# V cast into DRAM and loaded by SyncE; batch 1's global rows gathered one by one

## The chip, the cores and the metric

One core of a Trainium2 chip runs the whole kernel in one launch. The metric is the device time of that launch in microseconds. The kernel before took 402.18 us (median of three runs, 399.71 to 402.31).

## The reference

Sparse attention, followed by a two-layer feed-forward block with a "snake" activation:

```
scores = (q @ k^T) / sqrt(64)                    # q, k, v: 8 batches, 8 heads, 576 rows, 64 columns
mask   = |i - j| <= 32, or i is global, or j is global      # 8 global rows, given by global_idx
attn   = softmax(where(mask, scores, -1e9));  x = attn @ v  # x: 4608 tokens of 8 * 64 = 512
h      = x @ w_in                                # 512 -> 2048
g      = h + sin(alpha * h)**2 / (alpha + 1e-9)
out    = g @ w_out                               # 2048 -> 512, float32
```

## The kernel before

**Per batch.** `attention(b)` goes over four pairs of heads (`hp`; a pair is head hp and head 4 + hp, on the two halves of the partitions). For a pair it makes band scores in two halves (`scores`, L785, into the bank `ring`), an exponential on ScalarE (L794), a mask on VectorE (L795), the products of the weights with V (`products`, L823, key 0) and with ones (key 1, the row sums), and divides by way of a logarithm: ScalarE writes `L` (L849), SyncE stores a row of it to `LC` (L851), ScalarE makes the inverse (L858) and VectorE multiplies into `xT` (L861). `L` has two buffers. The products of a pair are two steps behind its scores. `gemm1(b)` multiplies `xT` with `w_in` in 16 groups of 128 columns (L1014), with sine (L1044), square (L1047 or L1049) and the sum into `H2` (L1050). `gemm2(b)` is a generator of single matmuls with `w_out` (L1062); `fill(n)` takes n of them wherever TensorE would otherwise have a gap: `START`, `FIRST` and `SECOND` say how many at the start of an attention and after the first and second half of a pair, `PER_GROUP` and its like how many in a group of `gemm1`. After 16 of them ScalarE copies a block to `osb` (L1068, three buffers) and SyncE stores it (L1075).

**Order.** Each engine works through its instructions in the order of the program, and a wait holds up all that stands behind it on that engine. The order is written out by hand: attention 0, then for each batch b the first GEMM of b and the attention of b + 1, in which the second GEMM of b fills the gaps. `beside(at)` places other work after pair `at` of an attention. A DMA is issued by POOL (its own queue, q0, which can also cast), SyncE or ScalarE (hardware queues, q1 and q10).

**What is loaded.** Keys and queries of batch b are cast to bfloat16 in DRAM by POOL (`cast_qk`, L322, the tiles `kd` and `qd`, two buffers each) and turned by SyncE's transposing DMA (`turn_qk`, L331, into `kt` and `qt`); VectorE copies them into `KX` and `QX` (`place`, L341 and L348), for batches 1 and 2 in groups 10 to 13 of the first GEMM. Batch 0 is loaded as it is and turned by TensorE. V rows go straight into `VX` by POOL's casting DMA (`load_v`, L400), 32 transfers of 168 rows a batch; for batches 0 and 1 two of the pairs are staged in float32 by SyncE (`stage_v`, L389) and cast by POOL (L393). `VX` holds 48 V rows and 8 rows of the global keys in each group of partitions; `load_vg` (L405) fills in the latter.

**Global rows.** For batch 0 three indirect DMAs of POOL (L560) fetch 64 rows each of v, k and q. For all others SyncE fetches them by `gather` (L503): eight row indices are loaded into registers (L499), and 24 transfers with a register in the address bring the rows of all batches for k, q and v. POOL casts them (`cast_kq`, L715, and `cast_globals_v`, L711, into `VGb`), TensorE turns keys and queries (`turn_kq`, L727), and POOL copies each batch's columns into `KX` and `QX` (`place_globals`, L360 and L364). `gather(k)` and `gather(q)` stand in the set-up, ahead of batch 1's `turn_qk`; `gather(v)` behind it.

**POOL and SyncE around batch 1.** POOL: `w_in` in two halves with `cast_qk(1)` in between, `cast_kq`, a tiny copy into `seen` that waits for `kt`, V of pair 0, `w_out` in four transfers, then (in program order in group 10 of the first GEMM) `cast_globals_v`, `place_globals(1)`, V of pair 1 and the casts of the staged pairs 2 and 3, then `cast_qk(2)` and V of batch 2. SyncE: the gathers of k and q, `turn_qk(1)`, the gather of v, the staging of pairs 2 and 3, `load_vg(1)`, the logarithm stores, `turn_qk(2)`.

The last part checks bounds on the inputs of sine and logarithm and would call `general_path` where they don't hold.

Of the kernel before, what the change touches and what calls it, by code (L numbers as in the profile page):

```python
# [246 lines left out]
def kernel(  # L247
# [56 lines left out]
    VG0 = main.tile([NG * B, D], DT.bfloat16, name="VG0")  # L304
    seen = main.tile([1, 1], DT.bfloat16, name="seen")
    girow = main.tile([1, NG], DT.int64, name="girow")
    grow = main.tile([NG * B, 1], DT.int32, name="grow")
    grow2 = main.tile([P, 1], DT.int32, name="grow2")
# [8 lines left out]
    def cast_qk(b):  # L317

        cast[b] = []
        for src, name in ((k, "kd"), (q, "qd")):  # L320
            t = dramp.tile([P, H * S * D // P], DT.bfloat16, name=name)
            nc.gpsimd.dma_start(  # L322
                out=t[:], in_=src[b].rearrange("h s d -> (h s d)").rearrange("(p f) -> p f", p=P)
            )
            cast[b].insert(0, t)

    def turn_qk(b):

        turned[b] = [trp.tile([P, H * HALF], DT.bfloat16, name=name) for name in ("qt", "kt")]
        for i in (1, 0):  # L330
            nc.sync.dma_start_transpose(  # L331
                out=turned[b][i][:], in_=cast[b][i][:].rearrange("p (r c) -> (p r) c", c=P)
            )
        del cast[b]
# [49 lines left out]
    def stage_v(b, hp, st):  # L384


        for t in range(2):
            for r, src in v_rows(b, t * NHP + hp):
                nc.sync.dma_start(out=st[r : r + 24, :, t, :], in_=src)  # L389
# [5 lines left out]
    def load_v(b, hps=range(NHP)):  # L395
        for hp in hps:
            for t in range(2):
                h = t * NHP + hp
                for r, src in v_rows(b, h):
                    nc.gpsimd.dma_start(out=VX[b % 2][r : r + 24, :, h, :], in_=src)  # L400

    def load_vg(b):
        src = VGb[b::B] if b else VGd[:]
# [15 lines left out]
    def load_w_out():  # L419
        for g in range(4):  # L420
# [11 lines left out]
    GKQ = [H2[0 : NG * B, nt, S : S + H * D] for nt in (0, 12)]  # L432
# [106 lines left out]
    nc.vector.tensor_copy(out=grow[:], in_=rowf[0 : NG * B, 4:5])  # L539
    for e in range(2):  # L540
# [81 lines left out]
    def place_global_keys(t, copy):  # L622
        copy(
            out=KX[0][t * D : (t + 1) * D, :, :, KT:NK],
            in_=pg[1][:].rearrange("p (j t h) -> p t h j", t=2, h=NHP)[:, t][:, :, None, :].to_broadcast(
# [4 lines left out]
    def place_global_queries(t, copy):  # L630
        for y in range(2):
            copy(
                out=globals_of(0, slice(t * D, (t + 1) * D), y),
                in_=pg[0][:].rearrange("p (x y t h) -> p t y h x", t=2, h=NHP, y=2)[:, t, y][
# [15 lines left out]
    load_registers()  # L650
    gather(k, gk)
    gather(q, gq)
# [52 lines left out]
    stage1 = [  # L705
# [522 lines left out]
```

## Time and profile before

| | |
|---|---|
| Three runs | 402.31, 402.18, 399.71 us |
| Profiled execution | 398.96 us, span 397.2 us |
| Busy, share of the span | TensorE 85%, VectorE 69%, ScalarE 68%, POOL 47% |
| Mean granted TensorE clock | 0.959 |
| POOL's V transfers (L400) | 224 issues, 141.8 us busy |
| DMA queue q0 (POOL) | 58176 packets, 18.67 MB, 41.6% of 16 engines' span |
| DMA queue q1 (SyncE) | 47210 packets, 20.54 MB, 25.8% |

The span is from the first to the last instruction; the time has some 1.8 us around it. Busy time of TensorE is that of matmuls. A row of the list of waits gives who waited, for whom, then the microseconds in total, how often, and the longest. A row in order of time gives start and duration in microseconds, engine (SPq is SyncE's queue), line, operation, what is written and read, how many were merged, and in brackets the idle time before and what ended it. A row of a queue gives packets, megabytes and the time that the packets took as a share of 16 engines in the stretch.

### The profile page before, as it was taken

What the parts mean: (1) busy time and instruction counts of PE and PEld (TensorE: products, weight loads), DVE (VectorE), ACT (ScalarE), POOL (GpSimd) and SP (SyncE); (2) the same over time, 40 slices, a digit from 0 to 9 for tenths busy, and PEclk for the clock granted to TensorE, in tenths of its full rate; (3) what the DMA queues carried; (4) which work ended last, traced back from release to release, by engine and by line L of the source; (5) the groups of instructions that cost most, each with busy time, mean ns of one, the idle gap of its engine ahead of it and who ended that gap; (6) DMA issues with size and microseconds to landing.
All of it is one profiled execution on the core that took longest, in us unless ns stands there. A gap on an engine that the chain in (4) does not pass through costs nothing. (4 is left out here: it accounts for less than half of the span.)

```text
span 397.2 us, 11426 instructions
## 1 busy us (share of the span) xinstructions
PE 336.1 (85%) x4564; PEld 209.6 (53%) x4564; DVE 274.9 (69%) x521; ACT 269.7 (68%) x387; POOL 185.2 (47%) x300
## 2 busy tenths in 40 slices
PE   1576955299979999989999999899999998999990
PEld 1554633146645565556555755466556555665450
DVE  3554884247868788958897889588968785768520
ACT  1566893168777778768877797588787876777510
POOL 7880186657967958948749905980000000000001
PEclk9998995589999999999999999899999999999997
DMA  7999789899899898979966994596111011001221
GB/s 121 106 154 183 122 110 188 127 169 129 103 182 133 114 177 92 133 123 129 127 131 68 139 160 70 65 71 108 56 31 29 2 55 31 27 28 54 61 85 35
DMA packets 105463, 40.03 MB, mean 101 GB/s; under 512 B 96075, under 2 KB 99035, under 8 KB 104955
## 3 DMA queue, kind: packets, MB, share of 16 engines
q0 software_dynamic: 58176, 18.67, 41.6%
q1 hardware_dynamic: 47210, 20.54, 25.8%
q8 instruction: 38, 0.62, 0.6%
q14 instruction: 23, 0.18, 0.1%
q10 hardware_dynamic: 16, 0.02, 0.0%
HBM read 38.84 MB, written 17.83 MB: 143 GB/s over the span
## 5 line engine op out<-in xcount | busy, mean ns | idle before, releaser
L400 POOL DMA_DIRECT2D VX<-in_v_dram x224 | 141.8, 662 | 55.7 <-PE zn L823 26.3
L1062 PE MATMUL zo<-w_out,H 128*128 128x512 bf16 x576 | 153.6, 385 | 0.0
L1014 PEld LDWEIGHTS <-w_in 128*128 128x128 bf16 x1024 | 99.9, 98 | 52.2 <-issue 16.8
L794 ACT ACTIVATE E<-ring 128x720 bf16<-128x720 f32 x64 | 49.4, 772 | 40.5 <-PE ring L785 38.9
L1062 PEld LDWEIGHTS <-H 128*128 128x128 bf16 x576 | 51.1, 98 | 43.5 <-issue 1.8
L1014 PE MATMUL zn<-xT,w_in 128*128 128x288 bf16 (+1 forms) x384 | 57.4, 289 | 5.0 <-DVE H L1050 1.7
L1093 POOL DMA_INDIRECT out_dram<-osb,grow x1 | 1.1, 1057 | 123.3 <-SPq L1196 123.3
L1014 PE MATMUL zr<-xT,w_in 128*128 128x288 bf16 x320 | 47.8, 288 | 3.1 <-DVE GD L833 1.6
L1050 DVE SCALAR_TENSOR_TENSOR H<-s,recipT,zn 128x576 bf16<-128x576 bf16 (+1 forms) x48 | 39.5, 822 | 14.9 <-ACT s L1047 8.0
L1044 ACT ACTIVATE sb<-zn,alphaT 128x576 bf16<-128x576 f32 (+1 forms) x48 | 35.6, 741 | 20.4 <-PE zn L1014 20.2
L795 DVE TENSOR_TENSOR E<-E,MASK 128x720 bf16<-128x720 bf16 x64 | 35.9, 563 | 19.2 <-ACT E L794 18.3
L1014 PE MATMUL zd<-xT,w_in 128*128 128x288 bf16 x320 | 47.2, 291 | 0.7 <-DVE H L1050 0.6
L1047 ACT ACTIVATE s<-sb 128x576 bf16<-128x576 bf16 (+1 forms) x62 | 42.7, 689 | 2.0
L785 PEld LDWEIGHTS <-KX 64*64 64x64 bf16 x896 | 18.9, 116 | 44.0 <-issue 34.3
L785 PE MATMUL ring<-QX,KX 64*64 64x120 bf16 (+2 forms) x896 | 25.0, 228 | 19.5 <-POOL QX L364 9.0
L1049 DVE TENSOR_TENSOR s<-sb 128x576 bf16<-128x576 bf16 (+1 forms) x66 | 31.8, 481 | 10.9 <-ACT sb L1044 10.5
L1050 DVE SCALAR_TENSOR_TENSOR H<-s,recipT,zd 128x576 bf16<-128x576 bf16 (+1 forms) x40 | 32.9, 821 | 8.0 <-ACT s L1047 6.2
L1050 DVE SCALAR_TENSOR_TENSOR H<-s,recipT,zr 128x576 bf16<-128x576 bf16 (+1 forms) x40 | 32.9, 822 | 5.2 <-ACT s L1047 2.9
L1044 ACT ACTIVATE sb<-zd,alphaT 128x576 bf16<-128x576 f32 (+1 forms) x40 | 29.6, 741 | 8.2 <-PE zd L1014 7.2
L1044 ACT ACTIVATE sb<-zr,alphaT 128x576 bf16<-128x576 f32 (+1 forms) x40 | 29.6, 740 | 7.1 <-PE zr L1014 7.1
L823 PEld LDWEIGHTS <-VX 56*64 56x64 bf16 x896 | 18.4, 113 | 20.5 <-issue 18.1
L1068 ACT COPY osb<-zo 128x512 f32<-128x512 f32 x36 | 20.9, 581 | 11.3 <-PE zo L1062 11.2
(141 smaller groups left out, 323.2 us busy)
## 6 DMA issues: line engine op xcount, KB each, us to landing
VX<-in_v_dram POOLq DMA_DIRECT2D x224, 21.0 KB, 3.2
kd<-in_k_dram POOLq DMA_DIRECT2D x7, 576.0 KB, 6.1
qd<-in_q_dram POOLq DMA_DIRECT2D x7, 576.0 KB, 9.6
w_in<-in_moe_w_in_dram POOLq DMA_DIRECT2D x4, 512.0 KB, 13.8
w_out<-in_moe_w_out_dram POOLq DMA_DIRECT2D x4, 512.0 KB
out_dram<-osb SPq DMA_DIRECT2D x8, 256.0 KB
out_dram<-osb SPq DMA_DIRECT2D x8, 224.0 KB
out_dram<-osb SPq DMA_DIRECT2D x8, 192.0 KB
```

Source lines behind the costliest of these rows:

```text
L400: nc.gpsimd.dma_start(out=VX[b % 2][r : r + 24, :, h, :], in_=src)
L785: nc.tensor.matmul(out=zs[half * D : (half + 1) * D, t, 0 : G3 * WCOL].rearrange("p (m x c) -> p m x c", x=2, c=60)[:, m % G3, :, c0:c1], ...
L794: nc.scalar.activation(out=Eg, in_=zs[:, :, 0 : G3 * WCOL], func=AF.Exp, scale=scale)
L795: nc.vector.tensor_tensor(out=Eg, in0=Eg, in1=MASK[:, None, G3 * g : G3 * (g + 1), :].rearrange("p o m c -> p o (m c)").to_broadcast([P, 2 ...
L823: nc.tensor.matmul(out=nd(hp, key)[t * D : (t + 1) * D, half, :, a - half * CUT : z - half * CUT], lhsT=ones[rows, 0:D] if key else VXb[ro ...
L1014: nc.tensor.matmul(out=h_part, lhsT=w_in[:, c, nt * P : (nt + 1) * P], rhs=xT[:, c, lo:hi], start=(c == 0), stop=(c == CT - 1), skip_group ...
L1044: nc.scalar.activation(out=sb[:, 0:W], in_=h, func=AF.Sin, scale=alphaT[:, nt : nt + 1])
L1047: nc.scalar.activation(out=s2[:, 0:W], in_=sb[:, 0:W], func=AF.Square)
L1049: nc.vector.tensor_tensor(out=s2[:, 0:W], in0=sb[:, 0:W], in1=sb[:, 0:W], op=ALU.mult)
L1050: nc.vector.scalar_tensor_tensor(out=H2[:, nt, r0 : r0 + W], in0=s2[:, 0:W], scalar=recipT[:, nt : nt + 1], in1=h, op0=ALU.mult, op1=ALU.add,)
L1062: nc.tensor.matmul(out=ops[:], lhsT=H2[:, nt, blk * P : (blk + 1) * P], rhs=w_out[:, nt, :], start=(nt == 0), stop=(nt == NT - 1),)
L1068: nc.scalar.copy(out=osb[:], in_=ops[:])
```

## The change

V of batches 1 to 7 is cast to bfloat16 in DRAM beside keys and queries (`vd`, a third cast in `cast_qk`), and its rows are loaded from there by SyncE: for batch 1 pairs 0 and 1 (pairs 2 and 3 still by POOL from the float32 input, between the halves of `w_out`), for batch 2 all four pairs at the start of batch 1's first GEMM, for later batches one pair after each pair of the attention before. The float32 staging for batch 1 goes.

Batch 1's global rows come, like batch 0's, by three single indirect DMAs of POOL (`single_gathers(1)`, behind the second half of `w_in`); SyncE brings its V rows into the order needed by way of DRAM (`spread_vg(1)`, ahead of `turn_qk(1)` in its queue), TensorE turns keys and queries in group 7 of batch 0's first GEMM, and ScalarE and VectorE place them. The register loads and the 24 gathers for batches 2 to 7 stand behind batch 1's V and `load_vg(1)` on SyncE, ahead of `turn_qk(2)`; `cast_kq` comes after `turn_qk(2)` in the program, ahead of the casts for batch 3 on POOL, and `turn_kq` and `place_globals(2)` in group 6 of batch 1's first GEMM. The gathered rows lie in `spare2` instead of in `H2`, and the squares that share this buffer move from groups 3 and 4 to 6 and 7.

Batch 1's logarithm stores go to ScalarE's queue. Of the fills, three move from before an attention's first scores to behind them (`START` 4 to 1, `FIRST` 5 to 8).

```diff
-        for src, name in ((k, "kd"), (q, "qd")):
+        for src, name in ((k, "kd"), (q, "qd"), (v, "vd")):
...
-            cast[b].insert(0, t)
+            cast[b].append(t)
...
-                out=turned[b][i][:], in_=cast[b][i][:].rearrange("p (r c) -> (p r) c", c=P)
-            )
-        del cast[b]
+                out=turned[b][i][:], in_=cast[b][1 - i][:].rearrange("p (r c) -> (p r) c", c=P)
+            )
...
-    def v_rows(b, h):
+    def v_rows(src):
...
-                yield half * D + y * 24, v[b, h].rearrange("(m a y) d -> y a m d", a=24, y=2)[
+                yield half * D + y * 24, src.rearrange("(m a y) d -> y a m d", a=24, y=2)[
...
-            for r, src in v_rows(b, t * NHP + hp):
+            for r, src in v_rows(v[b, t * NHP + hp]):
...
-    def load_v(b, hps=range(NHP)):
+    def load_v(b, hps, queue):
+
+
+        src = v[b] if queue is nc.gpsimd else cast[b][2][:].rearrange("(h x) (s d) -> h (x s) d", h=H, d=D)
         for hp in hps:
-            for t in range(2):
-                h = t * NHP + hp
-                for r, src in v_rows(b, h):
-                    nc.gpsimd.dma_start(out=VX[b % 2][r : r + 24, :, h, :], in_=src)
+            for h in (hp, NHP + hp):
+                for r, rows in v_rows(src[h]):
+                    queue.dma_start(out=VX[b % 2][r : r + 24, :, h, :], in_=rows)
     def load_vg(b):
-        src = VGb[b::B] if b else VGd[:]
+        src = VGb[b::B] if b > 1 else VGd[b][:]
...
-    GKQ = [H2[0 : NG * B, nt, S : S + H * D] for nt in (0, 12)]
+    GKQ = [H2[0 : NG * B, nt, S : S + H * D] for nt in (14, 15)]
...
-    ]
-    gq, gk, gv = [
-        H2[0 : NG * B, nt, 0 : 2 * H * D].bitcast(DT.float32).rearrange("p (h d) -> p h d", d=D)
-        for nt in (13, 14, 15)
...
-    g0 = {}
-    for name, src in (("v", v), ("k", k), ("q", q)):
-        g0[name] = VG0 if name == "v" else setup.tile([NG * B, D], DT.bfloat16, name="g0" + name)
-        nc.gpsimd.indirect_dma_start(
-            out=g0[name][:], out_offset=None, in_=src[0].rearrange("h s d -> (h s) d"),
-            in_offset=bass.IndirectOffsetOnAxis(ap=grow[:, 0:1], axis=0),
-        )
-    load_v(0, (0, 1))
+    VGd = [dramp.tile([NG, H * D], DT.bfloat16, name=f"VGd{b}") for b in range(2)]
+
+    def single_gathers(b):
+
+
+        for i, src in ((2, v), (1, k), (0, q)):
+            nc.gpsimd.indirect_dma_start(
+                out=g01[:, b, i, :], out_offset=None, in_=src.rearrange("b h s d -> (b h s) d"),
+                in_offset=bass.IndirectOffsetOnAxis(ap=(grow, grow1)[b][:, 0:1], axis=0),
+            )
+
+    def spread_vg(b):
+        nc.sync.dma_start(out=VGd[b][:].rearrange("j (h d) -> (j h) d", d=D), in_=g01[:, b, 2, :])
+
+    single_gathers(0)
+    load_v(0, (0, 1), nc.gpsimd)
     nc.scalar.activation(out=qrel[:], in_=qrel[:], func=AF.Square, bias=kpos[:, 0:1], scale=-1.0)
-    VGd = dramp.tile([NG, H * D], DT.bfloat16, name="VGd")
-    nc.sync.dma_start(out=VGd[:].rearrange("j (h d) -> (j h) d", d=D), in_=VG0[:])
+    spread_vg(0)
...
+    def turn_single(b, z):
+
+
+        pg[b] = [z[:, w * NG * H : (w + 1) * NG * H] for w in range(2)]
+        for w in (1, 0):
+            nc.tensor.transpose(
+                out=pg[b][w], in_=g01[:, b, w, :], identity=identb[0 : NG * H, 0 : NG * H]
+            )
+
...
-    load_registers()
-    gather(k, gk)
-    gather(q, gq)
+    single_gathers(1)
+    spread_vg(1)
...
-    for w, name in ((1, "k"), (0, "q")):
-        pg[w] = both[0:D, 32 + w * 64 : 64 + w * 64].bitcast(DT.bfloat16)
-        nc.tensor.transpose(
-            out=pg[w][:], in_=g0[name][:], identity=identb[0 : NG * B, 0 : NG * B]
-        )
+    turn_single(0, both[0:D, 32:160].bitcast(DT.bfloat16))
     nc.tensor.transpose(out=both[:, 0:NT], in_=arow[:], identity=idf[0:NT, 0:NT])
     for t in range(2):
-        place_global_keys(t, act)
-        place_global_queries(t, act)
+        place_global_keys(0, t, act)
+        place_global_queries(0, t, act)
...
-    stage1 = [
-        spare2[:, n * NV : (n + 1) * NV].rearrange("p (m t d) -> p m t d", t=2, d=D) for n in range(2)
+    gk, gq, gv = [
+        spare2[0 : NG * B, n * H * D : (n + 1) * H * D].rearrange("p (h d) -> p h d", d=D) for n in range(3)
...
-        zt = zo[1].bitcast(DT.bfloat16)
+        zt = zo[1 - filling[0]].bitcast(DT.bfloat16)
...
-            (nc.sync if b else nc.scalar).dma_start(
+            (nc.sync if b > 1 else nc.scalar).dma_start(
...
-            if b == 1 and nt in (3, 4):
-                square_x(0, nt - 3)
-            if b == 0 and nt == 9:
+            if b == 1 and nt in (6, 7):
+                square_x(0, nt - 6)
+            if b == 0 and nt == 7:
+                turn_single(1, zo[1].bitcast(DT.bfloat16)[0:D])
+                for t in range(2):
+                    place_global_keys(1, t, nc.scalar.copy)
+                    place_global_queries(1, t, nc.vector.tensor_copy)
+            if b == 1 and nt == 0:
+                load_v(2, range(NHP), nc.sync)
+                cast_globals_v()
+                load_vg(2)
+            if b == 1 and nt == 6:
                 turn_kq()
-            if b == 0 and nt == 10:
-
-                cast_globals_v()
-                place_globals(1)
-                load_v(1, (1,))
-                for n in range(2):
-                    cast_v(1, 2 + n, stage1[n])
-                load_vg(1)
+                place_globals(2)
...
-    START = 4
-    FIRST, SECOND = (5, 5, 5, 5), (4, 4, 4, 3)
+    START = 1
+    FIRST, SECOND = (8, 5, 5, 5), (4, 4, 4, 3)
...
-                    cast_kq()
                     turn_qk(1)
+                    nc.gpsimd.tensor_copy(out=seen[:], in_=turned[1][1][0:1, 0:1])
+                    load_v(1, (0, 1), nc.sync)
+                    load_v(1, (2,), nc.gpsimd)
+                    load_w_out((0, 1))
+                    load_v(1, (3,), nc.gpsimd)
+                    load_w_out((2, 3))
+                    load_vg(1)
+                    load_registers()
+                    gather(k, gk)
+                    gather(q, gq)
                     gather(v, gv)
-                    nc.gpsimd.tensor_copy(out=seen[:], in_=turned[1][1][0:1, 0:1])
-                    load_v(1, (0,))
-                    load_w_out()
-                    for n in range(2):
-                        stage_v(1, 2 + n, stage1[n])
...
+                cast_kq()
+            if b_moe and b_att + 1 < B and 0 <= at < NHP:
+                load_v(b_att + 1, (at,), nc.sync)
...
-            load_v(b + 2, (0,))
-
+        if 1 < b < B - 1:
             place_globals(b + 1)
-            load_v(b + 2, range(1, NHP))
-            load_vg(b + 2)
-        elif 0 < b < B - 1:
-            place_globals(b + 1)
+            load_vg(b + 1)
...
-                load_v(2)
-                load_vg(2)
```

More of the change, by code (lines that the diff above doesn't have):

```diff
@@ L417, in load_w_in, with load_w_out @@
                 )
-    def load_w_out():
-        for g in range(4):
+    def load_w_out(gs):
+        for g in gs:
             nc.gpsimd.dma_start(
@@ L539 @@
     nc.vector.tensor_copy(out=grow[:], in_=rowf[0 : NG * B, 4:5])
+    nc.vector.tensor_scalar(
+        out=grow1[:], in0=rowf[0 : NG * B, 4:5], scalar1=float(H * S), scalar2=None, op0=ALU.add
+    )
     for e in range(2):
@@ L620, with place_global_keys @@
     pg = {}
-    def place_global_keys(t, copy):
+    def turn_single(b, z):
[4 more added lines that the diff above has]
+            )
+    def place_global_keys(b, t, copy):
         copy(
-            out=KX[0][t * D : (t + 1) * D, :, :, KT:NK],
-            in_=pg[1][:].rearrange("p (j t h) -> p t h j", t=2, h=NHP)[:, t][:, :, None, :].to_broadcast(
+            out=KX[b][t * D : (t + 1) * D, :, :, KT:NK],
+            in_=pg[b][1].rearrange("p (j t h) -> p t h j", t=2, h=NHP)[:, t][:, :, None, :].to_broadcast(
                 [D, NHP, NT12, NG]
@@ L628, in place_global_keys, with place_global_queries @@
         )
-    def place_global_queries(t, copy):
+    def place_global_queries(b, t, copy):
         for y in range(2):
             copy(
-                out=globals_of(0, slice(t * D, (t + 1) * D), y),
-                in_=pg[0][:].rearrange("p (x y t h) -> p t y h x", t=2, h=NHP, y=2)[:, t, y][
+                out=globals_of(b, slice(t * D, (t + 1) * D), y),
+                in_=pg[b][0].rearrange("p (x y t h) -> p t y h x", t=2, h=NHP, y=2)[:, t, y][
                     :, :, None, :
@@ L1096, in gemm2_globals @@
         )
-    waiting = []
+    waiting, filling = [], [0]
     def fill(n):
```

6 lines of the change are left out of this document (4 added, 2 removed).

## The prediction

> **What bounds the kernel now.** I read the page's head, then the list of waits, then TensorE's order of time around the longest ones.
>
> ```profile
> span 397.2 us, 11426 instructions
> PE 336.1 (85%) x4564; PEld 209.6 (53%) x4564; DVE 274.9 (69%) x521; ACT 269.7 (68%) x387; POOL 185.2 (47%) x300
> PEclk9998995589999999999999999899999999999997
> ```
>
> TensorE is busiest, and its clock is down only in slices 7 and 8, at 60 to 80 us. The list of waits (who, for whom: us, times, longest) names the place:
>
> ```profile
> PE ring L785 <- POOL QX L364: 9.0, 2, 6.5
> PE zn L823 <- DMA VX<-VGb: 7.4, 1, 7.4
> ACT L L849 <- DMA LC<-L: 4.1, 2, 2.5
> ```
>
> In order of time (start, duration, engine, line), TensorE's landmarks are:
>
> ```profile
> 45.19 1.14 PE L1014 MATMUL zr<-xT,w_in 128*128 128x288 bf16 x8
> ...
> 63.24 0.52 PE L785 MATMUL ring<-QX,KX 64*64 64x88 bf16 x14 [6.49 <-POOL QX L364]
> ...
> 77.01 1.19 PE L823 MATMUL zn<-E,VX 56*64 56x88 bf16 x28 [7.36 <-DMA VX<-VGb]
> ...
> 89.72 0.91 PE L1014 MATMUL zn<-xT,w_in 128*128 128x288 bf16 x6
> ...
> 117.44 0.35 PE L785 MATMUL ring<-QX,KX 64*64 64x88 bf16 x14 [2.50 <-POOL QX L364]
> ...
> 123.64 0.67 PE L823 MATMUL zn<-E,VX 56*64 56x88 bf16 x28
> ...
> 134.43 0.91 PE L1014 MATMUL zn<-xT,w_in 128*128 128x288 bf16 x6
> ```
>
> These are group 7 of batch 0's first GEMM, batch 1's first scores and first products with V, batch 1's first GEMM, then batch 2's scores, products and first GEMM. Batch 1 loses 6.5 us waiting for its global columns and 7.4 us for its global V rows; batch 2 loses 2.5. Later TensorE is the bound, as this stretch shows (us, PE busy, PEld, DVE, ACT, POOL, clock, DMA share, GB/s):
>
> ```profile
> 180.00:190.00 10.00, 10.00 (x76) 7.26 (x75) 8.24 (x14) 8.10 (x12) 8.18 (x14) 1.00 1.27 156
> ```
>
> So the change can win some 16 us at most, all before 120 us. What it loads instead is SyncE's queue:
>
> ```profile
> 18.32 0.64 SPq L405 DMA_DIRECT2D VX<-VGd  x2
> 24.12 12.75 SPq L503 DMA_DIRECT2D H<-in_k_dram  x8
> 37.07 6.84 SPq L503 DMA_DIRECT2D H<-in_q_dram  x8
> 44.02 2.08 SPq L331 DMA_TRANSPOSE kt<-kd  x1
> 46.20 3.46 SPq L331 DMA_TRANSPOSE qt<-qd  x1
> ...
> 56.83 15.71 SPq L389 DMA_DIRECT2D spare<-in_v_dram  x16
> 72.70 2.83 SPq L405 DMA_DIRECT2D VX<-VGb  x4
> ...
> 83.00 4.62 SPq L331 DMA_TRANSPOSE kt<-kd  x1
> ```
>
> **The change, part by part. Batch 1's start.** POOL now issues a V cast ahead of the second half of w_in, and the three single gathers behind it.
>
> ```profile
> 26.99 1.27 POOL L414 DMA_DIRECT2D w_in<-in_moe_w_in_dram  x2
> ...
> DMA to landing us min/median/max: 12.8/13.8/14.7
> DMA to landing us min/median/max: 5.4/6.1/8.9
> DMA to landing us min/median/max: 8.7/9.6/10.5
> ```
>
> The landings are those of w_in, kd and qd. The second w_in transfer lands at about 27.6 + 14.7 = 42.3 before. qd, issued right behind kd, lands 9.6 - 6.1 = 3.5 us later than kd: that is the price of one cast, and V's is the same size. So w_in lands at 45.8 and the gathered rows at about 47. Two things wait. TensorE's turn of these rows stands ahead of group 7, which began at 45.19: 1.8 us (from 0, if the rows slip past, to 4). And SyncE: spread_vg(1) waits for the rows with turn_qk(1) queued behind it, so batch 1's transposes start at 47.5 instead of 44.02; they take 5.7 us to 53.2. ScalarE's copies of the global keys add under 1 us; turn_kq, cast_globals_v and place_globals(1) leave this stage. Without their wait first scores would have begun at 63.24 - 6.49 = 56.75; with these delays it is about 60.
>
> V of pairs 0 and 1 is then 16 issues of SyncE, that of pairs 2 and 3 still 16 of POOL. Their prices (SyncE: least, median and most ns; POOL: busy us, mean ns):
>
> ```profile
> L389 SPq DMA_DIRECT2D H<-in_v_dram x16: 298/387/1108, 4.2 to 15.5; - x16
> L400 POOL DMA_DIRECT2D VX<-in_v_dram x224 | 141.8, 662 | 55.7 <-PE zn L823 26.3
> ```
>
> An unhindered issue on SyncE is 0.39 us, 0.42 with its gap; beside w_out's transfers sixteen took 15.71, or 0.98 each. Bounds 6.7 and 15.7 us; I take 0.5 (8 us), since w_out comes only towards the end: SyncE is at 61.2, the two transfers of global rows end at 62.5 and land, behind the last V rows, at 68 (72 by the upper bound). Products are wanted 77.01 - 7.36 - 63.24 = 6.4 us after the first scores, at 66.4, so they start at 68 instead of 77.01. From there to the first GEMM passed 12.7 us before; a clock that isn't halved gives back about 1: 80 instead of 89.72. **Gain so far 9.7 us** (5 to 11).
>
> **Where it goes: the gathers and batch 2's transposes.** The 24 row gathers now stand on SyncE behind all this, ahead of turn_qk(2). Eight register loads took from 18.96 to 24.12, 5 us; a gather takes 6.84 / 8 = 0.85, 24 of them 20.4 us. From 62.5 that is 88, later than the 83.00 of before though TensorE is 9.7 us ahead. And the casts are in the way. Records, MB and share of the two queues in three stretches of 2 us: 30 to 32 (casts on POOL's queue, gathers on SyncE's), 62 to 64 (w_out and V staging), 72 to 74 (V rows on both):
>
> ```profile
> q0 software_dynamic: 35, 0.46, 109.2%
> q1 hardware_dynamic: 20, 0.00, 1.6%
> ...
> q0 software_dynamic: 331, 0.33, 99.8%
> q1 hardware_dynamic: 225, 0.05, 20.9%
> ...
> q0 software_dynamic: 839, 0.07, 63.7%
> q1 hardware_dynamic: 888, 0.21, 61.2%
> ```
>
> While casts run, SyncE's queue moves 10 records a us, against 444 beside small packets. A batch's casts now take three times 3.5 = 10.5 us instead of 7. Casts for batch 2 follow V of pairs 2 and 3 and w_out on POOL's queue, which starts with kt(1) at about 52.5: 8 x 0.66 to 57.8, then w_out, 2 MB at 0.33 MB in 2 us (12.7 us), with 8 V transfers in its midst. So the casts run at about 75 to 85.5: the gathers of q stick, with eight transfers outstanding, and are done at about 90. Only then can POOL run cast_kq, with the casts for batch 3 queued right behind it: about 93 to 103.5, just when SyncE issues turn_qk(2) (95). Its keys land at about 105 (94 if nothing starves, 108 at worst). VectorE wants them at
>
> ```profile
> 106.41 0.91 DVE L348 COPY KX<-kt 64x1152 bf16<-64x1152 bf16 x2
> ```
>
> minus 9.7, so at 96.7: 8.4 us late, and behind that copy in VectorE's order stand the H columns of groups 10 to 15, for which TensorE's banks wait. The first GEMM ends at about 114; before, scores could have begun at 117.44 - 2.5 = 114.9. **Gain left: 1 us.**
>
> **Batch 2's V.** Behind the transposes SyncE issues 32 V transfers (32 x 0.42 = 13.4 us; 18 at 0.56) and only then the global rows (1.4). The casts of k and q for batch 4 wait for nothing but the DRAM buffers that turn_qk(2) has just read, so they run for 7 us beside V; eight issues fit into them, the rest follows: from 107 to 123, global rows landed at 126.5 (112 without starving, 131 at worst). Needed: 114 + (123.64 - 117.44) = 120.2. Batch 2's products at 126.5 instead of 123.64: **2.9 us behind.** (The 2.5 us wait for POOL's global columns is gone here, since place_globals(2) now comes at group 6 on a free POOL.)
>
> **Batch 2's attention.** The stores of a block and of a logarithm cost SyncE, and the logarithm of pair 2 runs, as in these rows:
>
> ```profile
> 158.98 0.80 SPq L1075 DMA_DIRECT2D out_dram<-osb  x2
> ...
> 163.25 0.56 SPq L851 DMA_DIRECT2D LC<-L  x1
> ...
> 130.05 0.65 ACT L849 ACTIVATE L<-zd 128x576 f32<-128x576 f32 x1
> ```
>
> SyncE has two stores, turn_qk(3) (5.7), a store and 8 V issues (3.4) ahead of batch 2's first logarithm store (about 2 to land, as V does): 124.4 + 15 = 139.5. L has two buffers, so pair 2's logarithm waits for that store; it would run at 130.05 + 2.9 = 133: 6.5 us late, and half a us more for pair 3. Bounds 0 (SyncE ahead) and 12 (the casts for batch 5 fall here too). TensorE reaches its next first GEMM at 126.5 + 10.8 + 7 = 144.3 instead of 134.43: **9.9 us behind.**
>
> **What costs nothing.** From batch 3 on, SyncE has per batch 13.4 us of V, about 8 of transposes and 8 of stores and global rows in some 40, and the casts fall beside the first GEMM; the cover is that V is wanted a batch later; were it gone, the logarithm wait would cost up to 5 us a batch. The moved fills keep their sum of nine before the second scores, which wait for ScalarE's table load and first exponential either way:
>
> ```profile
> 156.41 1.28 ACT L756 ACT_TABLE_LOAD   x1
> ...
> 158.53 0.35 PE L785 MATMUL ring<-QX,KX 64*64 64x120 bf16 x14 [0.82 <-ACT E L794]
> ```
>
> Later squares, another staging place and batch 1's logarithm stores on ScalarE's queue (four short issues where it waits anyway) move no end.
>
> **Sum.** The profiled execution took 398.96 (span 397.2): 398.96 - 9.7 + 8.7 + 3.9 + 7 = 408.9. The three runs lie 0.8 to 3.4 above that execution, so I say 410 for their median; its own range is 403 to 416.
>
> The Trainium skill, DMA: Bandwidth & Descriptors, section Queues, rings and completion order, says that an engine takes turns between rings packet by packet, and that a packet holds typically 9 to 17 descriptors. With cast packets of 16 x 2 x 1.09 / 35 = 1 us each, that would let SyncE's queue move some 150 to 270 rows a us, as an estimate by that page, and would leave the V loads nearly unhindered. The 20 records in 30 to 32 speak against more than one row a turn; what it would make of the time is the first rival.
>
> **Rivals.** *SyncE's queue keeps moving beside casts* (chance 0.22). Place: gathers of q and turn_qk(2). Then keys land at 94, before 96.7; V and the global rows at 112, wanted at 111.4; the logarithm store still costs about 6: 398.96 - 9.7 - 2.5 + 0.6 + 6 = 393.4. It decides if turn_qk(2) lands before 97. For it: 444 records a us beside small packets, and that one can't see how many gathers the 20 records held up. Against: the 12.75 us that the first eight gathers took where 6.84 would do is the same collision.
>
> *One collision only* (0.18): the casts for batch 3 come late enough to miss turn_qk(2), so 6 of the 8.7 us stay won and the logarithms wait less: about 401, no change. Against: cast_kq releases them at the wrong moment in every count that I made.
>
> *All of it bites* (0.12): V of batch 1 at 0.98, V rows of batch 2 at 131, 12 us of logarithm waits: 398.96 + 7.9 + 12 = about 419.
>
> *The change doesn't do what it says*: single gathers behind w_in are no earlier than 47, so batch 1's columns might miss their place; but 47 is still 14 us ahead of 61, so I give it nothing of its own.
>
> **How the numbers follow.** Forecast 0.48, rivals 0.22, 0.18, 0.12. One per cent, some 4 us, is about what a measurement of this kernel can tell from no change. Slower by more than that: most of the forecast and all of the last rival, 0.58; within it: the second rival and the forecast's edge, 0.19; faster: the first, with a little of the second, 0.23. The range 393 to 423 reaches from the first rival to the last, plus the runs' offset.
>
> **What would show it.** Right: batch 1's products near 68 us and its first GEMM near 80; then VectorE's copies from kt waiting for a transpose, TensorE's first product of batch 2 waiting for VX<-VGb, and ScalarE's L waiting for LC, together over 15 us, all before 150; SyncE's gathers between 65 and 95. Wrong: turn_qk(2) landed before 97, or the three waits under 5 us together; then the time is below 398. If batch 1's products are later than 72, the first step is already wrong.

## The result, and the profile after

The changed kernel took **425.5 us** (median of 4 runs, 423.39 to 426.18) against 401.43 for the kernel before beside it: a ratio of 1.060, 95% interval 1.054 to 1.065. It is slower, by 24 us; 410 was predicted, and 425.5 lies above the range. The profiled execution took 425.18 us, 26.2 more than the 398.96 of before. Span and busy times of its page:

```profile
span 423.5 us, 11374 instructions
PE 344.6 (81%) x4566; PEld 213.6 (50%) x4566; DVE 271.3 (64%) x526; ACT 270.9 (64%) x389; POOL 64.9 (15%) x111
PEclk9999986996698595999999999999999999999996
```

POOL's work has fallen from 185.2 to 64.9 us and no other engine's has grown by more than 8.5: the loss is mostly waiting. The 8.5 are TensorE's, whose clock is now down in places up to slice 16, 170 us, not 80 (eight matmuls of the GEMM took 2.08 us at 107.62, at a granted clock of 0.50, and 1.14 at 116.61, at 1.00). TensorE's landmarks in order of time (first scores, first products, first GEMM of a batch):

```profile
61.25 0.35 PE L797 MATMUL ring<-QX,KX 64*64 64x88 bf16 x14 [0.47 <-DVE H L1064]
...
68.63 1.00 PE L835 MATMUL zn<-E,VX 56*64 56x88 bf16 x28
...
82.61 0.91 PE L1026 MATMUL zn<-xT,w_in 128*128 128x288 bf16 x6
...
121.81 0.35 PE L797 MATMUL ring<-QX,KX 64*64 64x88 bf16 x14
...
141.20 0.35 PE L835 MATMUL zn<-E,VX 56*64 56x88 bf16 x2 [12.39 <-DMA VX<-VGb]
...
166.49 1.36 PE L1026 MATMUL zn<-xT,w_in 128*128 128x288 bf16 x5 [0.28 <-DVE GN L845]
...
188.94 0.35 PE L797 MATMUL ring<-QX,KX 64*64 64x88 bf16 x14
...
339.94 0.35 PE L797 MATMUL ring<-QX,KX 64*64 64x88 bf16 x14
```

The last two are the first scores of batches 3 and 7. Of the kernel before, the same two:

```profile
156.17 0.35 PE L785 MATMUL ring<-QX,KX 64*64 64x88 bf16 x14
...
314.96 0.35 PE L785 MATMUL ring<-QX,KX 64*64 64x88 bf16 x14
```

Against before the first GEMM of batch 1 is 7.1 us early, batch 2's scores are 4.4 late, its products 17.6, the first GEMM of batch 2 32.1, batch 3's scores 32.8; then four batches take 151.0 instead of 158.8 us and win 7.8 back. So there are three losses, all between 82 and 167, and one gain that the prediction did not have. The list of waits (who, for whom: us, times, longest) has a row for each loss:

```profile
ACT L L861 <- DMA LC<-L: 16.5, 3, 13.5
...
PE zn L835 <- DMA VX<-VGb: 12.4, 1, 12.4
PE zn L1026 <- DVE H L1064: 11.6, 4, 10.8
DVE spare L948 <- POOL VGb L723: 11.1, 1, 11.1
...
POOL VGb L723 <- DMA spare<-in_v_dram: 10.9, 1, 10.9
```

Read from the bottom, the last three are one chain: the gathered rows of v come late, POOL's cast of them into `VGb` waits, VectorE's square of batch 0's x (L948) waits for that cast, since it writes `spare2`, in which those rows are staged, and behind the square in VectorE's order stand the H columns (L1064) for which TensorE's banks wait. SyncE's and POOL's queues in order of time show why each transfer was late:

```profile
44.64 0.45 SPq L570 DMA_DIRECT2D VGd<-g  x1
...
64.69 14.70 SPq L501 DMA_DIRECT2D spare<-in_k_dram  x8
79.59 9.11 SPq L501 DMA_DIRECT2D spare<-in_q_dram  x8
88.89 6.76 SPq L501 DMA_DIRECT2D spare<-in_v_dram  x8
95.81 7.29 SPq L332 DMA_TRANSPOSE kt<-kd  x1
...
106.60 31.39 SPq L402 DMA_DIRECT2D VX<-vd  x32
138.07 1.41 SPq L407 DMA_DIRECT2D VX<-VGb  x2
```

```profile
91.54 0.49 POOL L323 DMA_DIRECT2D kd<-in_k_dram  x1
...
108.47 0.49 POOL L323 DMA_DIRECT2D kd<-in_k_dram  x1
...
111.66 0.49 POOL L323 DMA_DIRECT2D kd<-in_k_dram  x1
...
149.96 0.95 POOL L360 COPY KX<-kTg 128x384 bf16<-128x384 bf16 x1 [36.70 <-PE ring L797]
...
151.81 0.49 POOL L323 DMA_DIRECT2D kd<-in_k_dram  x1
```

The casts for batch 3 start at 91.5 over v's gather and kt; those for batch 4 **and** batch 5 at 108.5 and 111.7 over batch 2's V; those for batch 6 at 151.8 over the logarithm stores and batch 3's V.

### The profile page after: what moved, and what is told of

Read it like the earlier page. It is cut to its first block, busy times and chain, and to the rows that moved or that the text cites. A ratio compares the mean times of both kernels' runs of the same rounds, so it can differ in the third digit from the quotient of the medians.

```text
span 423.5 us, 11374 instructions
## 1 busy us (share of the span) xinstructions
PE 344.6 (81%) x4566; PEld 213.6 (50%) x4566; DVE 271.3 (64%) x526; ACT 270.9 (64%) x389; POOL 64.9 (15%) x111
## 5 line engine op out<-in xcount | busy, mean ns | idle before, releaser
L1026 PEld LDWEIGHTS <-w_in 128*128 128x128 bf16 x1024 | 102.8, 101 | 64.7 <-issue 26.4
L1026 PE MATMUL zn<-xT,w_in 128*128 128x288 bf16 (+1 forms) x384 | 59.9, 297 | 14.8 <-DVE H L1064 11.6
L1026 PE MATMUL zr<-xT,w_in 128*128 128x288 bf16 x320 | 51.4, 303 | 2.6 <-DVE H L1064 2.6
L1026 PE MATMUL zd<-xT,w_in 128*128 128x288 bf16 x320 | 48.1, 295 | 0.7 <-DVE H L1064 0.5
L1064 DVE SCALAR_TENSOR_TENSOR H<-s,recipT,zn 128x576 bf16<-128x576 bf16 (+1 forms) x48 | 39.4, 821 | 10.2 <-ACT s L1061 6.9
L1064 DVE SCALAR_TENSOR_TENSOR H<-s,recipT,zd 128x576 bf16<-128x576 bf16 (+1 forms) x40 | 32.8, 821 | 10.3 <-ACT s L1061 8.6
L1063 DVE TENSOR_TENSOR s<-sb 128x576 bf16<-128x576 bf16 (+1 forms) x66 | 30.9, 467 | 13.2 <-ACT sb L1058 12.8
L1083 ACT COPY osb<-zo 128x512 f32<-128x512 f32 x36 | 20.9, 580 | 26.6 <-DMA out_dram<-osb 13.9
L1064 DVE SCALAR_TENSOR_TENSOR H<-s,recipT,zr 128x576 bf16<-128x576 bf16 (+1 forms) x40 | 32.9, 821 | 7.8 <-ACT s L1061 4.6
L797 PE MATMUL ring<-QX,KX 64*64 64x120 bf16 (+2 forms) x896 | 24.8, 225 | 12.6 <-ACT E L806 10.1
L360 POOL COPY KX<-kTg 128x384 bf16<-128x384 bf16 x6 | 5.6, 932 | 157.7 <-PE ring L797 156.0
L835 PE MATMUL zn<-E,VX 56*64 56x120 bf16 (+2 forms) x672 | 17.1, 222 | 14.3 <-DMA VX<-VGb 12.4
## 6 DMA issues: line engine op xcount, KB each, us to landing
qd<-in_q_dram POOLq DMA_DIRECT2D x7, 576.0 KB, 10.8
```

Of the source, the lines that this page charges most:

```text
L360: nc.gpsimd.tensor_copy(out=KX[b % 2][:, :, :, KT:NK], in_=kTg[:, :, None, :, b].to_broadcast([P, NHP, NT12, NG]))
L797: nc.tensor.matmul(out=zs[half * D : (half + 1) * D, t, 0 : G3 * WCOL].rearrange("p (m x c) -> p m x c", x=2, c=60)[:, m % G3, :, c0:c1], ...
L835: nc.tensor.matmul(out=nd(hp, key)[t * D : (t + 1) * D, half, :, a - half * CUT : z - half * CUT], lhsT=ones[rows, 0:D] if key else VXb[ro ...
L1026: nc.tensor.matmul(out=h_part, lhsT=w_in[:, c, nt * P : (nt + 1) * P], rhs=xT[:, c, lo:hi], start=(c == 0), stop=(c == CT - 1), skip_group ...
L1063: nc.vector.tensor_tensor(out=s2[:, 0:W], in0=sb[:, 0:W], in1=sb[:, 0:W], op=ALU.mult)
L1064: nc.vector.scalar_tensor_tensor(out=H2[:, nt, r0 : r0 + W], in0=s2[:, 0:W], scalar=recipT[:, nt : nt + 1], in1=h, op0=ALU.mult, op1=ALU.add,)
```

## The experiments

"Before" in the ratios is the kernel before, run beside them on the same chip.

**e1: no casts from batch 3 on.**

```
 def cast_qk(b):
+    if b > 2: cast[b] = cast[2]; return
```

> Leaves out the casts into DRAM for batches 3 to 7; these batches read batch 2's tiles instead. All issues on SyncE stay. Theory A (casts starve SyncE's queue): batch 2's 32 V issues take 14 to 17 us instead of 31.4, TensorE's wait for VX<-VGb falls from 12.4 to under 3 us, the logarithm's wait for LC from 13.5 to 4 to 7, VectorE's wait for VGb from 11 to under 4; the median is 392 to 400. Rival B (SyncE's own number of issues, or 128-byte rows on its queue, is the bound): the V issues still take over 25 us, the three waits keep over half of their 37 us, and the median stays above 412.

Measured: 395.58 us, ratio 0.983 (0.976 to 0.990). Its list of waits, and SyncE in order of time:

```profile
ACT L L864 <- DMA LC<-L: 14.5, 5, 5.4
...
DVE spare L951 <- POOL VGb L726: 4.1, 1, 4.1
```

```profile
101.11 14.29 SPq L405 DMA_DIRECT2D VX<-vd  x32
...
126.94 3.43 SPq L405 DMA_DIRECT2D VX<-vd  x8
130.47 0.56 SPq L866 DMA_DIRECT2D LC<-L  x1
...
144.52 3.38 SPq L405 DMA_DIRECT2D VX<-vd  x8
147.99 0.51 SPq L866 DMA_DIRECT2D LC<-L  x1
```

V of batch 2 takes 14.3 us instead of 31.4 and TensorE's wait for it is gone: the casts make that loss, not SyncE's 32 issues. The time, within theory A's 392 to 400, agrees. The longest of the logarithm's waits falls from 13.5 to 5.4, as expected, but five of them make 14.5, hardly less than the 16.5 of the changed kernel. Without any cast the stores still stand between SyncE's own V issues of 3.4 us a pair.

**e2: the casts in rows of 512 elements.**

```
-out=t[:], in_=src[b]....rearrange("(p f) -> p f", p=P)
+out=..."(c p f) -> p c f", p=64, f=512, in_=... the same
```

> The casts move the same bytes in rows of 512 elements instead of one long piece per partition. Theory A in the form that the 16 engines take turns packet by packet: SyncE's queue moves 100 records a us or more while casts run, as beside w_out, instead of about 10; the LC wait falls from 13.5 to under 4 us, VectorE's wait for VGb from 11 to under 4, the V issues to some 27 us; the median is 405 to 414. Rival C (casts take the memory's bandwidth, whatever the size of their pieces): within 1% of the changed kernel, 421 to 430.

Measured: 417.71 us, ratio 1.038 (1.031 to 1.046), between the two. Records, MB and share of the two queues from 110 to 122, in the changed kernel and then in e2:

```profile
q0 software_dynamic: 198, 2.49, 99.1%
q1 hardware_dynamic: 175, 0.02, 1.8%
```

```profile
q0 software_dynamic: 2231, 2.22, 109.8%
q1 hardware_dynamic: 1475, 0.42, 24.0%
```

With cast records of 1.0 KB instead of 12.6 KB, SyncE's queue moves 1475 instead of 175 in the same 12 us, and in both it moves somewhat under one record for each of the casts'. So the size of the casts' records sets the starving, as a turn-taking of whole records would have it. Rival C, the memory's bandwidth, does not fit: the casts' own rate is nearly the same in both. V of batch 2 still took 26.8 us (27 expected), as the small records also prolong the casts (2.22 instead of 2.49 MB in these 12 us), and TensorE still waited 12.3 for it; the waits for `VGb` (7.6) and for `LC` (longest 8.7) fell less than expected (under 4).

**e3: each batch's casts held until the attention of two batches earlier is done.**

```
+if b > 1:
+    nc.gpsimd.tensor_copy(out=seen[:], in_=xTs[b][0:1, NHP - 1, 0:1])
 cast_qk(b + 2)
```

> One tiny POOL copy that reads the end of attention b's output stands ahead of the casts for batch b + 2 from b = 2 on, so that they run beside the first GEMM and not beside batch 2's V. Nothing is left out. Theory A: V issues of batch 2 take 14 to 17 us, the waits for VX<-VGb and LC fall below 3 us each, VectorE's wait for VGb (11 us) stays; the median is 397 to 404. Rival B: above 415. Rival D (casts that come later make batch 3's keys late instead): VectorE waits for kt in attention 2, the median 408 or more.

Measured: 407.04 us, ratio 1.015 (1.008 to 1.023).

```profile
105.79 14.53 SPq L402 DMA_DIRECT2D VX<-vd  x32
```

V of batch 2 in 14.5 us, no wait for it, longest logarithm wait 4.2: the place of the casts from batch 4 on is worth some 18 us. The time is above theory A's 397 to 404, as the batches from 3 on took 39.0 us instead of 37.75. Rival D's reason for a longer time does not show: VectorE's list has no wait for kt here. In these four batches TensorE waits 5.3 us for VectorE's H columns, 0.2 in the changed kernel; why VectorE is later there stays open. The wait for `VGb` stayed at 9.1, as the casts for batch 3 were not moved.

**e4: the gathered rows of v in a part of `spare2` that the squares do not write.**

```
-gk, gq, gv = [spare2[..., n * H * D : (n + 1) * H * D] ... n in range(3)]
+gk, gq, gv = [spare2[..., n : n + H * D] ... n in (0, H * D, 2 * NV - H * D)]
```

> The gathered global V rows lie in a part of spare2 that the squares don't use, so that the square of batch 0's x no longer waits for cast_globals_v. Theory A: the 11 us wait moves on to VectorE's copies from kt(2), which land at about 105 us against some 98 wanted, so batch 2's first scores move from 121.8 to 116 to 120 and the products keep waiting for V's global rows until 141: the median stays within 1% (422 to 428). Rival E (the shared buffer was the loss): the median falls by 8 us or more, below 418.

Measured: 424.48 us, ratio 1.055 (1.047 to 1.063), as expected. Batch 2's scores come at 116.18 instead of 121.81, its products at 141.22, where they were:

```profile
PE zn L835 <- DMA VX<-VGb: 17.3, 1, 17.3
...
DVE KX L348 <- DMA kt<-kd: 5.2, 2, 3.8
```

The shared buffer's wait stood ahead of V's, which ends later whatever is done here; and kt, now waited for 5.2 us, had only been hidden behind it.

**e5: batch 2's V by GpSimd, straight from its source.**

```
-load_v(2, range(NHP), nc.sync)      # first GEMM of batch 1
+load_v(2, range(NHP), nc.gpsimd)    # behind cast_qk(2)
```

> The changed kernel, but batch 2's V goes as before: 32 row loads straight from in_v by GpSimd's queue, issued right behind the casts for batch 2 (at about 70, where GpSimd then waits 20 us for the gathered queries), and no vd for batch 2. Theory A (the 31.4 us in which SyncE issues V(2) beside two batches' casts are what holds batch 2's products): TensorE's wait VX<-VGb (12.4) goes below 2, VectorE's wait for VGb (11) stays, batch 2's products begin at 126 to 130 instead of 141.2, the logarithm's wait for LC falls below 6, and the time is 400 to 408. Rival B (the casts hold whatever else SyncE has to bring at that place, so the wait only moves on to LC, to the output's store or to kt): products still gain, but the time is 412 to 422.

Measured: 410.66 us, ratio 1.021 (1.015 to 1.026): between the two again. Products at 126.50, as theory A had it, 14.7 us earlier; but the transposes for batch 3 now met the casts (the first took 16.75 us to issue), and with them the logarithm's store, a wait of 9.9. Part of the gain moved on, as rival B had it.

**e6: e5, and the casts for batch 3 behind batch 2's transposes, later ones behind the global columns.**

```
+place_globals(b + 1); load_vg(b + 1)     # b from 2
 cast_qk(b + 2)
-place_globals(b + 1); load_vg(b + 1)
 # in the first GEMM of batch 1:
+nc.gpsimd.tensor_copy(out=seen[:], in_=turned[2][0][0:1, 0:1]); cast_qk(3)
```

> As the run before, and the casts are moved: those for batch 3 wait for batch 2's turned queries (about 103 instead of 91.5) and stand behind VGb's cast; from batch 4 on each batch's casts stand behind the copies of the global columns of the batch before it, not ahead of them, so that GpSimd cannot issue two batches' casts in a row (batch 5's come at the end of batch 2's scores, not at 112). Theory A (starved transfers on SyncE's queue are all of the loss): no wait of over 3 us for VGb, kt, VX<-VGb or LC; batch 2's scores at 113 to 116, its products at 120 to 123, first GEMM of batch 2 at 135 to 138, steady batches of 37.7 to 38.2 us, time 394 to 400: faster than before. Rival D (casts cost something wherever they run, as the paced casts did at 39.0 us a batch): steady batches of 39 us and a time of 402 to 408.

Measured: 406.7 us, ratio 1.008 (1.004 to 1.013): not faster than before, and within rival D's 402 to 408. It does not decide between the two, since the waits that theory A wanted gone are still in its trace (an execution of 413.34 us): 9.2 us for `VGb` and up to 7.6 for the logarithm's store. The casts for batches 3 and 4 again came 5.4 us apart (104.7 and 110.1), and the first transpose for batch 3, behind them, took 11.2 us to issue. From batch 4 on a batch takes 37.8 us there, not D's 39.

**e7: e6, with V of all batches from 2 on by GpSimd.**

```
-load_v(b_att + 1, (at,), nc.sync)
+load_v(b_att + 1, (at,), nc.gpsimd)
```

> As the run before, but V of batches 3 to 7 is also loaded straight from in_v by GpSimd's queue, at the places where the changed kernel has SyncE's loads, and V is cast into DRAM for batch 1 alone. It asks where the changed kernel's 37.75 us a batch (39.7 before) come from. Theory P (V's route: loads by GpSimd beside an attention slow it): 39.2 to 40.2 us a batch and 5 to 9 us more than the run before. Rival Q (the gain is the moved fills' or the removed waits' elsewhere): 37.7 to 38.3 us a batch, within 2 us of the run before.

Measured: 399.31 us, ratio 0.995 (0.991 to 0.998). Neither theory: it is 7.4 us faster than e6, not slower, and its batches take 38.5 us. What it cures is the logarithm's store: with no V on SyncE the four stores of batch 2 go out without V between them, and its list of waits has no row for `LC`.

```profile
127.07 0.56 SPq L863 DMA_DIRECT2D LC<-L  x1
...
130.60 0.53 SPq L863 DMA_DIRECT2D LC<-L  x1
...
134.17 4.05 SPq L863 DMA_DIRECT2D LC<-L  x2
```

e7 alone does not say that V's place cured it: with V's loads back in POOL's order the casts also stand apart again (105.9, 133.4, 162.9), two a batch instead of three. But e1, with V on SyncE and no casts at all, still has 14.5 us of these waits. Together they say that the third loss has two parts: casts, and V ahead of the stores in SyncE's order.

**e8: the fills as before.**

```
-START, FIRST = 1, (8, 5, 5, 5)
+START, FIRST = 4, (5, 5, 5, 5)
```

> The changed kernel with the fills as before (START 4 and 5, 5, 5, 5 instead of START 1 and 8, 5, 5, 5). Theory N (the moved fills neither gain nor lose): 423.5 to 427.5 us and 37.6 to 37.9 us a steady batch. Rival F (they are the source of the shorter steady batches): 38.5 to 39.7 us a batch and 429 to 434 us.

Measured: 425.01 us, ratio 1.057 (1.051 to 1.063), 37.8 us a batch. The moved fills neither gain nor lose here; rival F falls.

**e9: the gathers of k and q early, as before.**

```
 load_w_in((1,))
+load_registers(); gather(k, gk); gather(q, gq)   # into H's tiles 13, 14
 single_gathers(1)
 ...
 load_vg(1)
-load_registers(); gather(k, gk); gather(q, gq)
 gather(v, gv)
```

> The changed kernel, but the gathers of the global rows of k and q go where they stood before: behind the first half of w_in on SyncE's queue (SyncE has nothing to issue from 19 to 44), into H's tiles 13 and 14, with their casts ahead of batch 1's transposes; only v's gather stays behind batch 1's V. Theory M (the squares waited because k's and q's gathers, 24 us of SyncE's queue from 64.7 to 88.9, stood ahead of v's, and so pushed it into the casts for batch 3): v's rows are asked for at 59 to 67 and VectorE's wait for VGb (11.1) goes below 1, kt(2) is asked for before 85, batch 2's scores begin at 110 to 116 instead of 121.8; if batch 2's V is then still beside casts, its products wait and the time is 408 to 420, if not 400 to 408. Rival E2 (the wait only moves to batch 2's V, as it did when gv had a place of its own): products at 139 to 142 again and 421 to 426 us.

Measured: 418.44 us, ratio 1.042 (1.038 to 1.045). Now v's rows are asked for at 62.2 and kt(2) at 82.6, VectorE's wait for `VGb` is gone, and batch 2's scores begin at 111.40, 10.4 us earlier: theory M is right on the squares. But casts follow each other here too: those for batches 2 and 3 (71.8 and 73.3) stand over kt, those for 4 and 5 (99.2 and 102.4) over V, as before:

```profile
82.62 13.81 SPq L332 DMA_TRANSPOSE kt<-kd  x1
...
100.56 30.58 SPq L402 DMA_DIRECT2D VX<-vd  x32
131.25 1.41 SPq L407 DMA_DIRECT2D VX<-VGb  x2
```

Products at 134.39 after a wait of 15.1. Of the 10.4 us 6.8 reach the products: rival E2's 139 to 142 is wrong too.

**e10: e7 with e9's early gathers.** `VGb`'s cast and batch 2's global rows of V stand in group 10 of batch 0's first GEMM, as before.

```
 # e7 and e9 together, and
-cast_globals_v(); load_vg(2)    # group 0 of batch 1
+cast_globals_v(); load_vg(2)    # group 10 of batch 0
```

> The run with all later V by GpSimd (V of batches 2 to 7 from in_v, casts later), and the gathers of k and q early as in the run above, VGb's cast and batch 2's global rows of V at group 10 of batch 1's... first GEMM (that of batch 0's rows) as before. What it keeps of the change is batch 1: single indirect gathers, V through the cast copy for its first two pairs, the moved fills. Theory M: no wait over 2 us for VGb, kt, VX or LC; batch 2's scores at 110 to 114, its products at 117 to 121, first GEMM of batch 2 at 129 to 133, 38.2 to 38.8 us a batch: 386 to 393 us. Rival (the 8 us ahead in batch 1 are lost again to casts or to GpSimd's 64 V issues before batch 2 ends): first GEMM of batch 2 at 135 or later, 396 to 402 us.

Measured: **393.05 us, ratio 0.977 (0.973 to 0.981)**: faster than both kernels. Batch 2's scores at 111.50 and products at 118.34 as theory M had it; its first GEMM at 133.57 and the time are just above the upper ends, and its batches take 39.2 us (38.2 to 38.8 expected).

```profile
POOL VX L402 <- PE zn L841: 25.0, 2, 14.5
POOL VGb L729 <- DMA spare<-in_v_dram: 8.9, 1, 8.9
...
ACT L L867 <- DMA LC<-L: 5.7, 2, 2.9
```

The wait for the rows of v is still there, but VectorE no longer stands behind it. It is 5.3 us ahead of the kernel before at batch 2's products (123.64 there), and 0.9 at its first GEMM (134.43).

**e11: e10, with V of batches 4 to 7 through DRAM and SyncE.**

```
-load_v(b_att + 1, (at,), nc.gpsimd)
+load_v(b_att + 1, (at,), nc.gpsimd if b_att == 2 else nc.sync)
```

> As the run before, but V of batches 4 to 7 comes as in the changed kernel, cast into DRAM and loaded by SyncE. Theory S (that route saves 0.7 us a batch against GpSimd's, as 37.75 against 38.5 us showed, once a batch has no late transposes on SyncE): 37.7 to 38.0 us a batch from batch 4 on and 1 to 4 us less than the run before. Rival T (the first batch with the route pays once with waits for LC of 5 us or more, as batch 2 did even with the casts left out): the same time or up to 5 us more than the run before.

Measured: 394.47 us, ratio 0.980 (0.974 to 0.987), the same as e10. From batch 4 on a batch takes 37.9 us (scores at 197.69 and 311.42), theory S's rate; but batch 3 takes 42.1 (from 155.62), and in that stretch VectorE waits 5.0 us for transposed keys. So the entry is paid, as rival T had it, though in another wait than it named. Here too two batches' casts come together, those for 4 and 5 at 138.0 and 141.3, and the first transpose behind them takes 13.9 us to issue.

**e12: batch 5's casts not beside batch 2's V.**

```
-cast_qk(b + 2); place_globals(b + 1); load_vg(b + 1)
+place_globals(b + 1); load_vg(b + 1); cast_qk(b + 2)    # b from 2
```

> The changed kernel with one order swapped: from batch 2 on GpSimd copies the global columns of batch b+1 first and then issues the casts for batch b+2. The copies for batch 4 wait for the end of batch 2's scores, so batch 5's casts cannot come at 112, right behind batch 4's: they come at 135 to 152. It asks how much of batch 2's loss is the second batch of casts beside its V, which the prediction had not counted. Theory H (the prediction's mechanism with one batch of casts was right, the second one made the rest): V(2) issued by 121 to 126, products limited by their own scores at 128 to 131 (scores stay at 121 to 122), TensorE's wait VX<-VGb below 2, first GEMM of batch 2 at 143 to 152 instead of 166.5, and 404 to 412 us. Rival (one batch's casts are enough to hold the 32 loads for most of the time): the wait stays above 8, 417 to 424 us.

Measured: 417.33 us, ratio 1.036 (1.030 to 1.042): the rival's lower end by its time, between the two by V's wait.

```profile
ACT L L861 <- DMA LC<-L: 17.6, 4, 13.2
...
PE zn L835 <- DMA VX<-VGb: 4.3, 1, 4.3
```

```profile
106.19 23.20 SPq L402 DMA_DIRECT2D VX<-vd  x32
129.48 1.41 SPq L407 DMA_DIRECT2D VX<-VGb  x2
...
146.51 9.88 SPq L402 DMA_DIRECT2D VX<-vd  x8
156.48 0.56 SPq L863 DMA_DIRECT2D LC<-L  x1
```

The second batch of casts is worth 8.2 us of V's issue (31.4 to 23.2) and 8.6 of the products (141.20 to 132.62); the first batch of casts costs 8.9 against e1's 14.3. Batch 5's casts, now at 142.5, meet the logarithm's store instead (9.9 us for eight V issues ahead of it), so that wait stays.

## Why the prediction was right and wrong

The direction and its reason held: batch 1 is ahead, and casts that starve SyncE's queue take that and more. By its own steps, what the first GEMM of batch 1 or the later landmark had won (-) or lost (+), against before:

| step | predicted | measured | from |
|---|---|---|---|
| batch 1's start | -9.7 | -7.1 | 89.72 to 82.61 |
| gathers and batch 2's transposes | +8.7 | +14.0 | 114.94 (scores without their wait) to 121.81: 6.9 behind |
| batch 2's V | +3.9 | +10.7 | 123.64 to 141.20: 17.6 behind |
| batch 2's attention | +7 | +14.5 | 134.43 to 166.49: 32.1 behind |
| from there to the end | 0 | -5.9 | 26.2 in all |

**Batch 1's start: right.** The gathered rows' store went out at 44.64 (47 predicted), products began at 68.63 (68), the first GEMM at 82.61 (80); the gain of 7.1 lies within the bounds of 5 to 11. (The page before has the clock at 8 tenths in slices 4 and 9 too, beside 7 and 8; nothing in the sum hangs on that.)

**Gathers and transposes: right on the queue, wrong on who waits.** SyncE asked for kt(2) at 95.8 (95), but it was not VectorE's copy that waited. "Later squares, another staging place ... move no end" is the sentence that failed: the squares write the buffer in which v's rows are staged, their cast stood behind the casts for batch 3 in the starved queue, and the 11.1 us came ahead of kt's and hid it. e9 shows it (wait gone, scores 10.4 us earlier); e4 shows kt's own wait behind it, 5.2, and scores 5.6 us earlier without the squares' wait.

**Batch 2's V: the mis-sized term that set the products.** Its rows were to be there at 126.5; the products began at 141.20, 14.7 us later. e4, with scores 5.6 us earlier, leaves them there, so up to this point it is V that sets the miss, however the table divides it. The mechanism was right: e1 and e3 bring the 32 issues to 14.3 and 14.5 us, near the 13.4 of the sum. But the prediction let casts run 7 us beside V, those of k and q for batch 4 alone, and with eight issues inside them this added only 2.6 us. All three of batch 4 ran, and added 8.9 (e12's 23.2 against e1's 14.3). Those of batch 5 ran 3.2 us behind them, and added another 8.2 (31.4 against e12's 23.2).

The prediction held casts back by the DRAM buffers alone. With two buffers for each tile, batch 5's casts would have had to wait until the transposes for batch 3 had read theirs, behind V on SyncE. The trace shows no such wait: those transposes went out at 141.48, the casts at 111.66, and POOL's queue had moved all of them by 128. As built, the program gives every batch DRAM tiles of its own. POOL's order has nothing between the two batches' casts but the copies of the global columns for batch 3, which had nothing to wait for, as the first that waits is the one for batch 4 (36.7 us, at 149.96). What had kept them apart were V loads between two batches' casts on POOL, which the diff removes: before, the casts went out at 77.5, 105.8 and 134.7, and in e7, with V's loads back on POOL, at 105.9, 133.4 and 162.9.

**Batch 2's attention: 14.5 instead of 7.** The prediction's bound of 12 named the cause, casts that fall on the store, and is itself too low. From the first products to the next first GEMM it took 25.3 us, 10.8 before. In e1, without casts, it takes 14.6, and in e3, whose casts come later, 11.7: most of the 14.5 goes with the casts, and at most 3.8 with V ahead of the stores on SyncE. In e7, with V on POOL, it takes 11.7 as well, and no row for the store is left. That the casts which do the harm are batch 6's in the changed kernel and batch 5's in e12 rests on the order of time alone.

**From batch 3 on: not nothing, but a gain.** A batch takes 37.75 us instead of 39.7. It is not the fills (e8). V's route gives 0.8 of the 1.95 (e7, with V by GpSimd again, takes 38.5; e11's fall from e10's 39.2 to 37.9 has the same sign). Of the other 1.15 us a batch some 0.6 come from one batch of the kernel before: it took 41.4 us at a granted clock of 0.96, the other three 38.5 to 39.8 at 1.00. Where the rest comes from stays open.

**The rivals.** "SyncE's queue keeps moving beside casts" is refuted by 15 records a us; "one collision only" by three losses; "all of it bites" at 419 came nearest. It had batch 2's V rows at 131 (they came at 139 to 141) and 12 us of logarithm waits (16.5); its first part is refuted, as SyncE issued batch 1's 16 V loads in 6.99 us, 0.44 each and not 0.98. "The change doesn't do what it says" is refuted by batch 1's start. Turns packet by packet, which the Trainium skill states in DMA: Bandwidth & Descriptors, section Queues, rings and completion order, agree with the records of the changed kernel and of e2, 0.9 and 0.7 of SyncE's for each of the casts'; its 9 to 17 descriptors a packet do not show for these rows, which moved at most about one for each of the casts' records.

## What to carry to other kernels

Before a load is rerouted through another queue, list what else the DMA engines carry in that stretch, and with which record size: here long casting records on one queue held a queue of short rows to about one record for each of theirs. When work is taken off an engine's order, ask what it had kept apart: here GpSimd's V loads had spaced the casts, and with them gone two batches' casts came at once. And a staging buffer in a shared tile is a wait; a step that "only moves" should be followed to everything that reads or writes its bytes. What the change does for batch 1 can be had without the rest: e10 keeps it and takes 393.05 us, though most of that lead is gone again by batch 2's first GEMM.

## What the runs showed of the hardware

Beside casts in records of 12.6 KB, a queue of row loads moved 15 records a us (175 in 12 us); beside the same casts in records of 1.0 KB it moved 123 (1475 in 12 us), while the casts' own rate fell only from 2.49 to 2.22 MB. SyncE's 32 row loads take 14.3 to 14.5 us unhindered, 0.45 each, 23.2 beside one batch's three casts and 31.4 beside two.
